# Attention and two MLPs on one core: PSUM banks held in pairs, weight pieces of 512 words, first scores one batch ahead, and MLP2's down weights decoded in the second phase

## The chip, the cores and the metric

One core of a Trainium2 chip runs the whole program. The metric is the device time of one execution in microseconds; lower is better. The kernel before was measured at 1560.72 us, the median of two executions (1560.45 and 1561.00).

## The reference, cut to what matters

```python
def sm_attn(qq, kk, vv):                    # scale = 1/8
    s = scale * np.matmul(qq, kk.transpose(0, 1, 3, 2))
    s = s - np.max(s, axis=-1, keepdims=True)
    a = np.exp(s)
    a = a / (np.sum(a, axis=-1, keepdims=True) + 1e-09)
    return np.matmul(a, vv)

p_packed = sm_attn(p, k, v)                 # 32 packed rows a head
out = sm_attn(q, p_packed, p_packed)        # (8, 8, 576, 64)

x = out.transpose(0, 2, 1, 3).reshape(4608, 512)
g = x @ w_gate                              # MLP1, d_ff 1536
x = (g * (1 / (1 + np.exp(-g))) * (x @ w_val)) @ w_out
h = x @ w_in                                # MLP2, d_ff 2048
y = (h * np.cos(h)) @ w_out2
```

The weights of both MLPs are float64. They arrive as pairs of 32-bit words and are turned into float32 on the chip. Where a product must keep float32's precision, an operand is split into a high and a low half (`split`: ACT copies to the high one, DVE subtracts to get the low one), and three matmuls replace one (`PASSES`).

## The kernel before, in words

**First phase, eight batches `b`.** `a_up(b)` (line 423) makes MLP1's gated hidden values for the 576 tokens of batch b: 12 columns `f` of 128 hidden units, each in two halves `c` of 288 tokens. A half has a gate product `pg` and a value product `pv`, in a bank of PSUM each (one pool `ps` of 8 banks). ACT evicts `pg` with silu (line 471), DVE multiplies it with `pv` into `h` (472), and POOL issues the store of `h` for both halves (479). The weights are multiplied with the packed values before (`a_wp`, line 408: two of the six 256-column groups `m` at a time, at f = 2, f = 6 and, for the next batch, in a side slot), so that the second attention's probabilities `a` can be multiplied with them directly. Batch 0 has no split operands and decodes the gate and value weights as it goes (`u_step`).

After every half a side slot `k = 2f + c` runs what the table `sched` holds. There are: the first scores of batch b+2 (`s1_mm` to `a_ppt`: p k^T, exp, times v, transposed), the second scores of batch b+1 (`s2_mm` to `s2_split`: q against the packed rows, softmax, split into `a`), loads of k, q, v, and `w2_step`: one step of the decode of the other weights, in pieces of 256 words. A piece is loaded by SP (`raw`, 328), decoded by two ACT operations (`w2t`, `w2f`: 98, 99) and two of DVE (105, 108), combined for Strassen's scheme (346), split (86, 87), and stored by SP (340) to `w1u` (MLP1's down weights), `w2u` (MLP2's up weights), and last to `w2d` (MLP2's down weights). The side slots of the last batch run two steps each. Engines work in program order, so what stands in a slot stands in front of the evictions behind it.

**Second phase.** MLP1's down product, as Strassen's seven products for each of five `SETS` of tokens (four with N = 512, one with N = 256). `prep` splits h (`hr`) into three `g` pieces for the next product (7 buffers); `sums1` makes differences of h quarters on DVE (534); `strassen(s_, i, m)` issues 18 matmuls for each half m, all three pieces `fp` for m = 0, then for m = 1, and `evict` adds up. DVE runs `sums1`, the low halves and the additions in that order. PE takes 7 x 36 matmuls a set.

**Third phase.** MLP2, whose functions `product`, `chain` and `down` the change does not touch.

Of the kernel before, what the change touches and what calls it, by code (L numbers as in the profile page):

```python
# [23 lines left out]
HS = S // 2  # L24
NP1 = NF1 // 2
NW1 = 2 * NP1
SETS = ((0, 512), (1024, 512), (2048, 512), (3072, 256), (3584, 512))
NC = -(-S // 128)
# [5 lines left out]
ATT = 24  # L34
ORDER = (0, 4, 6, 1, 3, 2, 5)
# [9 lines left out]
def attention_mlp_kernel(ctx: ExitStack, tc: tile.TileContext, qT, kT, vP, pP, wgv, w12, out):  # L45
# [5 lines left out]
    stage = {n: ExitStack() for n in ("ups", "att", "gates", "da", "db", "dw")}  # L51
# [7 lines left out]
    ps = ctx.enter_context(tc.tile_pool(name="ps", bufs=8, space=bass.MemoryType.PSUM))  # L59
# [11 lines left out]
    def wt(shape, dt, name):  # L71
        return ups.tile(shape, dt, tag="w", name=name, bufs=8)

    def bank(shape, name):
        return ps.tile(shape, F32, tag="b", name=name)
# [12 lines left out]

    def raw_words(alloc, src, n):
        r = alloc([128, n, 2], U32, "raw")  # L90
        SP.dma_start(out=r, in_=src.bitcast(U32).rearrange("p (n t) -> p n t", t=2))
        return r
# [19 lines left out]
    def keep_busy(n):  # L112
        wm = bank([128, 128], "wm")
        for _ in range(n):
            PE.matmul(out=wm, lhsT=zero, rhs=zero, start=True, stop=True)  # L115
# [26 lines left out]
    def pp_of(b, r, c):  # L142
        e, c1 = c % 2, 2 * (c // 2) + r
        return ppT[b, e][rows(r), cols(c1)]
# [3 lines left out]
    def s1_mm(b):  # L148
        sp = s1_["sp"] = [[bank([128, HS], "s1") for _ in range(2)] for _ in range(2)]
        for h in range(2):  # L150
            for c in range(4):
                for r in range(2):
                    PE.matmul(
                        out=sp[h][r][cols(c), :],
# [7 lines left out]
    def s1_max(r):  # L162
        mx = st.tile([128, 2], F32, tag="mx", name="mx")
        for h in range(2):
            DVE.tensor_reduce(out=mx[:, h:h + 1], in_=s1_["sp"][h][r], axis=AX.X, op=ALU.max)
        nm = s1_["nm", r] = st.tile([128, 1], F32, tag="nm", name="nm")
        DVE.tensor_scalar(
            out=nm, in0=mx[:, 0:1], scalar1=mx[:, 1:2], scalar2=-0.125, op0=ALU.max, op1=ALU.mult
        )

    def s1_exp():
        sp = s1_.pop("sp")
        for r in range(2):
            E[r] = at_([128, SPAD], F32, "E")
            nc.gpsimd.memset(E[r][:, S:SPAD], 0.0)
            sm = s1_["sm", r] = st.tile([128, 2], F32, tag="sm", name="sm")
            nm = s1_.pop(("nm", r))
            for h in range(2):
                ACT.activation(  # L179
                    out=E[r][:, HS * h:HS * h + HS], in_=sp[h][r], func=AF.Exp, scale=0.125,  # L180
                    bias=nm, accum_out=sm[:, h:h + 1],
                )

    def s1_sum():
        for r in range(2):
            rs[r] = st.tile([128, 1], F32, tag="rs", name="rs")
            sm = s1_.pop(("sm", r))
            DVE.tensor_scalar(
                out=rs[r], in0=sm[:, 0:1], scalar1=sm[:, 1:2], scalar2=1e-9, op0=ALU.add, op1=ALU.add
            )  # L190
            DVE.reciprocal(out=rs[r], in_=rs[r])

    def a_t():
        for r in range(2):
            e = E.pop(r)
            ET[r] = []
            for c0, n in ((0, 3), (3, 2)):
                tp = bank([128, n, 128], "tp")
                for c in range(n):
                    o = 128 * (c0 + c)  # L200
                    PE.transpose(out=tp[:, c, :], in_=e[:, o:o + 128], identity=ident)
                et = at_([128, n, 128], F32, "ET")
                ACT.activation(out=et, in_=tp, func=AF.Copy)
                ET[r].append(et)

    def a_pp(b):
        for r in range(2):
            et = ET.pop(r)
            pp = bank([128, 1, 64], "pp")
            for c in range(NC):  # L210
                for i in range(4):
                    PE.matmul(
                        out=pp[cols(i), 0, :],
                        lhsT=et[c // 3][:, c % 3, cols(i)],
# [5 lines left out]
                out=ppu[r], in0=pp.to_broadcast([128, 2, 64]), scalar1=rs.pop(r), scalar2=None, op0=ALU.mult  # L220
# [4 lines left out]
    def a_ppt(b):  # L225
# [799 lines left out]
```

## Time and profile before

| | us |
|---|---|
| median of two executions | 1560.72 |
| profiled execution | 1558.54 |
| its span | 1556.7 |
| PE busy in it | 1475.7 (95%) |
| DVE busy | 1117.6 (72%) |
| ACT busy | 866.0 (56%) |

A row of the trace gives start and length in us, engine, line, operation, tiles as out<-in, and in brackets how long the engine was idle before and what released it. SPq is SP's DMA queue, where the time is that of issuing. PEld are weight loads, which run beside the matmuls. The clock of PE is given as a share of its full speed. The stretches named here are: prologue to 24.9 us, batch 0 to 107.4, batches 1 to 6 to 431.4, the last batch to 508.0, the second phase to 802.0 (its first two products to 544.7), then the third phase.

### The profile page before, as it was taken

The page shows a single profiled execution, that of the slowest core. Times are in us where ns is not written, and L with a number is a line of the kernel's source. Part 1 is how long each engine was busy: PE and PEld are TensorE (multiplying, and loading weights), DVE is VectorE, ACT ScalarE, POOL GpSimd, SP SyncE. Part 2 cuts the span into 40 slices and gives each one's busy share as a digit, 9 for nine tenths or more (in the row PEclk, how much of TensorE's full clock was granted, in tenths as well). Part 3 has the DMA queues.
Part 4 walks back from the last instruction along what each step waited for, and adds up shares of the span by engine and source line. Part 5 has one row for each costly group of instructions (what it writes and reads, how often), then busy time and mean ns, then how long its engine had stood idle before and what let it go on. Part 6 is the DMA issues. An engine that isn't in the chain of part 4 may idle for free.

```text
span 1556.7 us, 26541 instructions
## 1 busy us (share of the span) xinstructions
PE 1475.7 (95%) x9452; PEld 1271.4 (82%) x9452; DVE 1117.6 (72%) x2139; ACT 866.0 (56%) x1847; POOL 76.3 (5%) x158
## 2 busy tenths in 40 slices
PE   9978999998966699999989999999999999999999
PEld 6657787787865588889888898999999999999987
DVE  6768898898855577677777676776686677577664
ACT  6766667667644343344447565555464655555552
POOL 0101111111100000001000000000000000000000
PEclk9999999999988899999999999999999999999999
DMA  9936787786678951535268666567558557656551
GB/s 344 344 118 234 257 308 262 275 288 231 212 260 269 321 196 65 210 112 185 89 243 285 209 197 226 184 213 256 168 180 286 189 165 245 225 185 190 191 164 45
DMA packets 160626, 335.72 MB, mean 216 GB/s; under 512 B 16880, under 2 KB 35312, under 8 KB 160496
## 3 DMA queue, kind: packets, MB, share of 16 engines
q1 hardware_dynamic: 149872, 296.28, 56.9%
q0 software_dynamic: 10624, 37.76, 6.2%
q8 instruction: 75, 1.23, 0.3%
q14 instruction: 55, 0.45, 0.1%
HBM read 252.71 MB, written 81.26 MB: 215 GB/s over the span
## 4 chain that ended last, share of the span: by engine, by line
PE 65%; issue 26%; POOL 3%; DVE 2%; ACT 2%; DMA 1%; POOLq 0%; SPq 0%; DVEq 0%; ACTq 0%
PE acc L888 25%; PE p L873 22%; PE o L557 16%; POOL h L479 3%; DMA hr<-h 0%; DMA raw<-in_wgv 0%; PE wm L115 0%; DMA h<-h 0%; PE pg L448 0%; PE pv L448 0%; DVE wg L105 0%; DVE xs L87 0%; ACT k L857 0%; ACT t L851 0%; ACT E L179 0%
## 5 line engine op out<-in xcount | busy, mean ns | idle before, releaser
L888 PE MATMUL acc<-wd,g 128*128 128x512 f32 x1728 | 418.1, 391 | 0.0
L873 PE MATMUL p<-xs,up 128*128 128x384 f32 x2016 | 381.3, 340 | 5.9 <-DMA up<-w2u 4.7
L873 PEld LDWEIGHTS p<-xs,up 128*128 128x128 f32 x2016 | 361.5, 189 | 17.5 <-issue 5.1
L888 PEld LDWEIGHTS acc<-wd,g 128*128 128x128 f32 x1728 | 323.1, 188 | 61.4
L557 PE MATMUL o<-g,w 128*128 128x512 f32 (+1 forms) x1260 | 267.4, 374 | 12.2 <-DVE g L87 10.5
L557 PEld LDWEIGHTS o<-g,w 128*128 128x128 f32 x1260 | 221.4, 190 | 57.9 <-DVE g L87 11.9
L851 ACT ACTIVATE t<-c,quarter 128x384 f32<-128x384 f32 x144 | 88.4, 614 | 200.8 <-DVE c L961 195.0
L463 PE MATMUL pg<-a,wp 128*128 128x288 f32 x1008 | 169.9, 304 | 28.6 <-ACT silu L471 14.9
L463 PEld LDWEIGHTS pg<-a,wp 128*128 128x128 f32 x1008 | 144.2, 191 | 54.1 <-ACT silu L471 20.0
L463 PE MATMUL pv<-a,wp 128*128 128x288 f32 x1008 | 163.9, 298 | 5.3 <-DVE h L472 4.3
L463 PEld LDWEIGHTS pv<-a,wp 128*128 128x128 f32 x1008 | 144.4, 190 | 8.5 <-DVE h L472 7.0
L86 ACT ACTIVATE g<-hr 128x1024 fp32r<-128x1024 f32 (+1 forms) x105 | 98.3, 968 | 70.6 <-DVE hr L534 46.5
L87 DVE TENSOR_TENSOR g<-hr,g 128x1024 fp32r<-128x1024 f32 (+1 forms) x105 | 113.3, 1113 | 22.4 <-ACT g L86 22.3
L956 DVE TENSOR_TENSOR u<-v,p 128x384 f32<-128x384 f32 x48 | 26.6, 554 | 121.1 <-PE p L873 120.8
L861 DVE TENSOR_TENSOR g<-t,g 128x384 fp32r<-128x384 f32 x192 | 106.0, 552 | 8.6 <-ACT g L848 8.5
L853 DVE TENSOR_TENSOR t<-t,k 128x384 f32<-128x384 f32 x192 | 106.1, 553 | 3.4 <-ACT k L857 1.8
L472 DVE TENSOR_TENSOR h<-silu,pv 128x288 f32<-128x288 f32 x192 | 85.8, 447 | 29.7 <-ACT silu L471 15.7
L471 ACT ACTIVATE silu<-pg 128x288 f32<-128x288 f32 x192 | 76.8, 407 | 46.6 <-PE pg L463 43.3
L854 ACT ACTIVATE t<-t 128x384 f32<-128x384 f32 x192 | 98.2, 512 | 2.5 <-DVE t L853 2.4
L848 ACT ACTIVATE g<-t 128x384 fp32r<-128x384 f32 x192 | 98.7, 514 | 0.4 <-DVE t L859 0.4
L902 DVE TENSOR_TENSOR oacc<-oacc,acc 128x512 f32<-128x512 f32 x108 | 73.8, 684 | 34.6 <-PE acc L888 34.6
L857 ACT ACTIVATE k<-t 128x384 int32<-128x384 f32 x192 | 98.0, 510 | 0.0
(97 smaller groups left out, 1504.5 us busy)
## 6 DMA issues: line engine op xcount, KB each, us to landing
up<-w2u SPq DMA_DIRECT2D x336, 256.0 KB, 3.1
wd<-w2d SPq DMA_DIRECT2D x96, 512.0 KB, 6.2
h<-h POOLq DMA_DIRECT2D x96, 288.0 KB, 4.0
hr<-h SPq DMA_DIRECT2D x48, 512.0 KB, 7.3
raw<-in_w SPq DMA_DIRECT2D x88, 256.0 KB, 4.0
w2u<-w2p SPq DMA_DIRECT2D x56, 256.0 KB, 3.6
raw<-in_wgv SPq DMA_DIRECT2D x24, 512.0 KB, 8.7
w1u<-w2p SPq DMA_DIRECT2D x42, 256.0 KB, 3.6
```

What stands on the lines that cost most here:

```text
L86: ACT.activation(out=hi, in_=src, func=AF.Copy)
L87: eng.tensor_tensor(out=lo, in0=src, in1=hi.bitcast(F32), op=ALU.subtract)
L463: PE.matmul(out=p_, lhsT=w[u][:, x, o:o + 128], rhs=a2[b, u][:, y, sl], start=(n == 0), stop=(n == 5),)
L557: PE.matmul(out=acc, lhsT=wd1[n, fp][:, j, 256 * x + 128 * m:256 * x + 128 * m + 128], rhs=g1[n, fp][:, y, j, :], start=(first and q == 0) ...
L848: ACT.activation(out=three["g"][:, 0, :], in_=three["t"], func=AF.Copy)
L851: ACT.activation(out=now["t"], in_=now["h"], func=AF.Identity, scale=1.0 / TWO_PI, bias=quarter)
L853: DVE.tensor_tensor(out=one_["t"], in0=one_["t"], in1=one_["k"], op=ALU.subtract)
L854: ACT.activation(out=one_["t"], in_=one_["t"], func=AF.Sin, scale=SIN_SCALE)
L857: ACT.activation(out=now["k"], in_=now["t"], func=AF.Copy)
L861: DVE.tensor_tensor(out=three["g"][:, 1, :], in0=three["t"], in1=three["g"][:, 0, :].bitcast(F32), op=ALU.subtract)
L873: PE.matmul(out=out, lhsT=w[:, u, 128 * k:128 * k + 128], rhs=x[:, v, k, :], start=(first and k == 0 and i == 0), stop=(last and k == 1 an ...
L888: PE.matmul(out=acc, lhsT=gs[p, a, t][:, x, o:o + 128], rhs=wd[j, f][:, y, :], start=(f == 0 and n == 0), stop=(f == 3 and n == 2),)
```

## The change

- **Bank pairs.** The pool `ps` holds four double banks [128, 2, 512]. `pg` and `pv` of both halves share one each, so one silu, one multiplication (128x576) evicts both; the same holds for scores, transposes and packed weights, and the second scores' softmax works on both 576-wide parts at once (128x1152). A group `m` of packed weights is made alone. The third phase opens a pool `ps1` of eight single banks.
- **Weight pieces of 512 words**, seven steps for a pair of pieces; their stores are issued by POOL, not SP. Batches 1 to 6 run 15 steps each, the last batch 8, all for `w1u` and `w2u`.
- **Scores one batch ahead.** `attention(sched, b + 1)` puts both scores of the next batch into batch b. The last batch and batch 0 hold no others.
- **MLP2's down weights** (16 items, 32 steps) are decoded in the second phase, one or two steps a product from product 3 of set 0 on.
- **Second phase.** The order of the products is 0, 4, 6, 1, 2, 3, 5; `strassen` takes the pieces `fp` outermost and both halves m within, into one double bank; `g` has 4 buffers; the loads of w1 and h and the three `prep` of product 0 are put into the last batch; the ten warm-up matmuls ahead of the phase leave. At the third phase's start the up weights take their tiles ahead of the down weights.

The core of the diff:

```diff
-ORDER = (0, 4, 6, 1, 3, 2, 5)
+ORDER = (0, 4, 6, 1, 2, 3, 5)
-    ps = ctx.enter_context(tc.tile_pool(name="ps", bufs=8, space=bass.MemoryType.PSUM))
+    ps = stage["ps"].enter_context(
+        tc.tile_pool(name="ps", bufs=4, space=bass.MemoryType.PSUM, reuse_waits="tile")
+    )
-    def bank(shape, name):
-        return ps.tile(shape, F32, tag="b", name=name)
+    def bank2(name):
+        return ps.tile([128, 2, 512], F32, tag="b", name=name)
...
+    def w2_put(w_, dst):
+        n = w_.shape[1]
+        p = w2_new([128, n, 2, 256], F32R, "p", "w2p")
+        split(w_, p[:, :, 0, :], p[:, :, 1, :])
+        nc.gpsimd.dma_start(out=dst.rearrange("n p c -> p n c"), in_=p.bitcast(F32).rearrange("p n x c -> p n (x c)"))
...
+        return [w2_decode(i), left, w2_decode(i + 1), sums_a, put_a, sums_b, put_b]
+
+    for n in range(NP1):
+        w2_todo += w2_pair(w1u[n], 2 * n)
+    for n in range(NPF):
+        w2_todo += w2_pair(w2u[n], NW1 + 2 * n)
+    for n in range(NF2):
+        w2_todo += [w2_decode(NW1 + NF2 + n), lambda n=n: w2_put_d(w2_f.pop(NW1 + NF2 + n), w2d[n])]
...
         for f in range(NF1):
+            pg = half(f, 0, "pg")
+            s_ = ups.tile([128, 2, HS], F32, tag="silu", name="silu", bufs=3)
+            ACT.activation(out=s_, in_=pg, func=AF.Silu)
+            side(2 * f)
+            pv = half(f, 128, "pv")
+            h_ = ups.tile([128, 2, HS], F32, tag="h", name="h", bufs=5)
+            DVE.tensor_tensor(out=h_, in0=s_, in1=pv, op=ALU.mult)
+            nc.gpsimd.dma_start(out=h1[f, :, S * b:S * b + S], in_=h_.rearrange("p c n -> p (c n)"))
+            side(2 * f + 1)
...
     def new_g(N):
-        n = g_n[0] % 7
+        n = g_n[0] % 4
...
         for fp in range(3):
-            for j in range(2):
-                for x, y in PASSES:
+            for m in range(2):
+                for j in range(2):
+                    for q, (x, y) in enumerate(PASSES):
...
+                for m, k in ((2, 2), (3, 5), (4, 9), (5, 14)):
+                    put(sched, k, lambda m=m: a_wp(b, m))
                 if b < B - 1:
+                    attention(sched, b + 1, (0, 1, 4, 4, 7, 8, 11, 12, 13, 13, 15, 16, 17, 18, 18, 21))
+                    for k in (1, 2, 3, 4, 5, 6, 7, 8, 9, 10, 19, 20, 21, 22, 23):
+                        put(sched, k, w2_step)
                 else:
-                    for k in range(24):
-                        put(sched, k, w2_step, w2_step)
-                    put(sched, 0, lambda: load_h(0, 0, 0), lambda: load_w1(0))
-                    put(sched, 6, lambda: load_h(0, 1, 0), lambda: load_h(0, 1, 1))
-                    put(sched, 20, lambda: prep(0, 0, 0))
-                    put(sched, 21, lambda: prep(0, 0, 1))
+                    for k in range(8):
+                        put(sched, k, w2_step)
+                    put(sched, 0, lambda: load_w1(0), lambda: g_first.append(new_g(512)), lambda: load_h(0, 0, 0))
+                    put(sched, 4, lambda: load_w1(4))
+                    put(sched, 8, lambda: load_h(0, 1, 0))
+                    put(sched, 12, lambda: load_w1(6))
+                    put(sched, 16, lambda: load_w1(1))
+                    for fp, k in enumerate((19, 21, 23)):
+                        put(sched, k, lambda fp=fp: prep(0, 0, fp))
...
-        prep(0, 0, 2)
-        load_w1(4)
-        load_w1(6)
+        load_h(0, 1, 1)
         load_h(0, 0, 1)
-        keep_busy(10)
         for s_ in range(len(SETS)):
             for i in range(7):
+                evict = strassen(s_, i)
                 sums1(s_, i)
+                for fp in range(3):
+                    prep(*nxt(s_, i), fp)
...
+                if s_ or i > 2:
+                    for _ in range(2 if i in (1, 6) else 1):
+                        w2_step()
...
+                evict()
```

Three places show what the change moves.

SP's DMA queue in the last batch, before: `raw` are loads of weight pieces, `w2d<-w2p` stores of decoded ones, `hr` loads of h for the second phase, `w_...<-w1u` loads of MLP1's down weights.

```order
L340 DMA w2d<-w2p 256x1x256
L505 DMA hr<-h_76 128x2x512 x3
L492 DMA w_6654<-w1u 128x2x512
L492 DMA w_6656<-w1u 128x2x512
L492 DMA w_6658<-w1u 128x2x512
L328 DMA raw<-in_w 128x512
L340 DMA w2d<-w2p 256x1x256
```

The same queue in the last batch of the change, up to the end of that batch, with the six loads of h that stand at the second phase's start as its last row:

```order
L513 DMA hr<-h_76 128x2x512 x3
L500 DMA w_5284<-w1u 128x2x512
L500 DMA w_5286<-w1u 128x2x512
L500 DMA w_5288<-w1u 128x2x512
L513 DMA hr<-h_76 128x2x512 x3
L500 DMA w_5459<-w1u 128x2x512
L500 DMA w_5461<-w1u 128x2x512
L500 DMA w_5463<-w1u 128x2x512
L500 DMA w_5539<-w1u 128x2x512
L500 DMA w_5541<-w1u 128x2x512
L500 DMA w_5543<-w1u 128x2x512
L513 DMA hr<-h_76 128x2x512 x6
```

Raw loads and stores have left the queue there.

ACT in the last batch, before: each silu has a weight piece's decode (98, 99) and split (86) in front of it.

```order
L471 ACTIVATE silu<-pg 128x288
L98 ACTIVATE w2t<-raw 128x256
L99 ACTIVATE w2f<-raw,low_87 128x256
L86 ACTIVATE w2p<-w2f 128x256
L86 ACTIVATE wp<-wp 128x512 x4
L471 ACTIVATE silu<-pg 128x288
L98 ACTIVATE w2t<-raw 128x256
```

ACT at the end of the last batch of the change: silus of 576 columns, the last packed weights (`wp`), and the splits of h for product 0 (`g`).

```order
L469 ACTIVATE silu<-pg 128x576
L86 ACTIVATE wp<-wp 128x2x512
L469 ACTIVATE silu<-pg 128x576 x3
L86 ACTIVATE wp<-wp 128x2x512
L469 ACTIVATE silu<-pg 128x576 x2
L86 ACTIVATE g<-hr 128x1024
L469 ACTIVATE silu<-pg 128x576
L86 ACTIVATE g<-hr 128x1024
```

No decode stands among the silus of the last two thirds any more.

DVE from the last batch's end into set 0 of the second phase, before: `h` is line 472, subtractions of h quarters are 534, low halves of `g` 87, evictions 577.

```order
L472 TENSOR_TENSOR h<-silu,pv 128x288 x2
L87 TENSOR_TENSOR g<-hr,g 128x1024
L534 TENSOR_TENSOR hr<-hr 128x1024 x3
L87 TENSOR_TENSOR g<-hr,g 128x1024 x5
L577 TENSOR_TENSOR x2e<-p,o_7520 128x512
L87 TENSOR_TENSOR g<-hr,g 128x1024
L577 TENSOR_TENSOR x2e<-p,o_7548 128x512
L534 TENSOR_TENSOR hr<-hr 128x1024 x3
```

The same place after the change: `h` is line 482, subtractions of h quarters are 542, evictions 575, weight steps 100 and 103 and `w2p`.

```order
L482 TENSOR_TENSOR h<-silu,pv 128x576
L87 TENSOR_TENSOR g<-hr,g 128x1024
L542 TENSOR_TENSOR hr<-hr 128x1024 x3
L87 TENSOR_TENSOR g<-hr,g 128x1024 x6
L575 TENSOR_TENSOR p<-p,o_5753 128x512 x2
L542 TENSOR_TENSOR hr<-hr 128x1024 x3
L87 TENSOR_TENSOR g<-hr,g 128x1024 x3
L542 TENSOR_TENSOR hr<-hr 128x1024 x3
L87 TENSOR_TENSOR g<-hr,g 128x1024 x3
L100 SCALAR_TENSOR_TENSOR w2f<-w2t,w2f 128x512
L103 SCALAR_TENSOR_TENSOR w2f<-raw,w2f 128x512
```

The three pieces of product 0 stand ahead of the phase's first subtractions now, and weight steps stand behind a product's three low halves.

## Rows read from the trace of the kernel before

**Rows 1.** Stretches: start:end, length, busy time of PE, PEld, DVE, ACT, POOL; clock; DMA; GB/s.

```profile
24.90:107.40 82.50, 71.95 (x681) 44.67 (x681) 59.77 (x120) 61.04 (x130) 6.57 (x15) 0.98 0.75 265
107.40:163.00 55.60, 51.68 (x544) 43.51 (x542) 45.30 (x111) 37.06 (x96) 6.44 (x14) 1.00 0.65 224
...
328.80:384.30 55.50, 51.58 (x543) 43.42 (x542) 48.53 (x122) 38.88 (x101) 6.75 (x15) 1.00 0.68 238
384.30:431.40 47.10, 46.54 (x419) 40.43 (x418) 41.89 (x98) 31.87 (x78) 6.23 (x12) 1.00 0.68 228
431.40:508.00 76.60, 49.67 (x353) 43.67 (x352) 39.12 (x93) 34.52 (x91) 6.49 (x12) 0.82 0.80 265
508.00:544.70 36.70, 23.54 (x93) 18.02 (x93) 19.31 (x25) 13.63 (x22) 1.62 (x3) 0.81 0.92 323
544.70:702.80 158.10, 158.10 (x685) 128.65 (x685) 116.46 (x112) 66.22 (x75) 11.90 (x22) 1.00 0.42 146
702.80:732.70 29.90, 29.90 (x254) 29.86 (x253) 24.89 (x41) 14.10 (x25) 4.12 (x8) 1.00 0.39 137
...
790.70:802.00 11.30, 6.59 (x23) 6.23 (x22) 4.67 (x7) 2.20 (x4) 0.55 (x1) 0.70 0.66 233
802.00:1556.70 754.70, 749.71 (x3725) 676.64 (x3723) 512.86 (x978) 417.80 (x886) 0.00 (x0) 1.00 0.62 204
```

**Rows 2.** Waits of PE in 431.4:508.0: waited for, us in total, times, longest.

```profile
PE pg L463 <- ACT silu L471: 14.5, 6, 12.0
PE pg L463 <- DVE wp L87: 11.9, 1, 11.9
```

**Rows 3.** Timeline of the last batch: start, length, engine, line, operation, idle before, releaser.

```profile
451.81 0.43 ACT L98 ACTIVATE w2t<-raw 128x256 f32<-128x256 f32 x1 [10.33 <-DMA raw<-in_w]
...
455.29 1.81 PE L463 MATMUL pg<-a,wp 128*128 128x288 f32 x6 [11.88 <-DVE wp L87]
...
479.73 0.43 ACT L98 ACTIVATE w2t<-raw 128x256 f32<-128x256 f32 x1 [11.13 <-DMA raw<-in_w]
...
482.29 1.81 PE L463 MATMUL pg<-a,wp 128*128 128x288 f32 x6 [12.02 <-ACT silu L471]
```

**Rows 4.** Timeline at the start of the second phase.

```profile
520.22 5.46 SPq L505 DMA_DIRECT2D hr<-h  x3
...
529.71 3.91 DVE L534 TENSOR_TENSOR hr<-hr 128x1024 f32<-128x1024 f32 x3 [10.76 <-DMA hr<-h]
...
534.81 5.41 PE L557 MATMUL o<-g,w 128*128 128x512 f32 x15 [8.94 <-DVE g L87]
```

**Rows 5.** Stretches: batches 1 to 6 in one row.

```profile
107.40:431.40 324.00, 304.96 (x3120) 257.67 (x3119) 280.40 (x688) 219.96 (x562) 39.62 (x81) 1.00 0.73 254
```

**Rows 6.** Instructions by line and shape: count, busy us, mean ns, idle before.

```profile
L472 DVE TENSOR_TENSOR h<-silu,pv 128x288 f32<-128x288 f32 x192 | 85.8, 447 | 29.7 <-ACT silu L471 15.7 <-PE pv L448 6.7 <-PE pv L463 5.3
...
L87 DVE TENSOR_TENSOR wp<-wp 128x512 fp32r<-128x512 f32 x84 | 52.0, 681 | 2.6 <-ACT wp L86 2.4
...
L87 DVE TENSOR_TENSOR a<-af,a 128x576 fp32r<-128x576 f32 x14 | 10.5, 752 | 1.5 <-ACT a L86 1.5
...
L87 DVE TENSOR_TENSOR g<-hr,g 128x1024 fp32r<-128x1024 f32 x84 | 99.7, 1220 | 20.3 <-ACT g L86 20.3
...
L87 DVE TENSOR_TENSOR g<-hr,g 128x512 fp32r<-128x512 f32 x21 | 13.7, 686 | 2.1 <-ACT g L86 2.0
...
L86 ACT ACTIVATE g<-hr 128x1024 fp32r<-128x1024 f32 x84 | 85.8, 1054 | 59.9 <-DVE hr L534 42.5 <-DMA hr<-h 10.6 <-PE o L557 5.1
...
L413 PE MATMUL wp<-wg,ppT 64*32 64x512 f32 x672 | 44.8, 597 | 7.1 <-ACT silu L471 7.1
...
L240 PE MATMUL s<-qt,ppT 64*32 64x288 f32 x256 | 10.4, 409 | 0.1
...
L471 ACT ACT_TABLE_LOAD x9 | 11.5, 1283 | 0.2
...
L179 ACT ACT_TABLE_LOAD x7 | 9.0, 1283 | 3.8 <-DVE nm L167 3.7
```

More of the change, by code (lines that the diff above doesn't have):

```diff
@@ L175, in s1_exp @@
             nc.gpsimd.memset(E[r][:, S:SPAD], 0.0)
[L176 to L182, printed above, removed]
+            sm = s1_["sm", r] = st.tile([128, 1], F32, tag="sm", name="sm")
+            ACT.activation(
+                out=E[r][:, :S].rearrange("p (h n) -> p h n", h=2), in_=sp[r][:, :, :HS], func=AF.Exp, scale=0.125,
+                bias=s1_.pop(("nm", r)), accum_out=sm,
+            )
     def s1_sum():
@@ new lines, in s2_back, with s2_split @@
+    def s2_back(b, u=None):
+        if "af" not in s2_:
+            s2_["af"] = att.tile([128, 2, S], F32, tag="af", name="af", bufs=2)
+        to, d_ = s2_["af"], s2_["d"]
+        if u is None:
+            DVE.transpose(out=to, in_=d_.rearrange("p (u a) n -> p u (a n)", u=2))
+        else:
+            DVE.transpose(out=to[:, u], in_=s2_d(u).rearrange("p a n -> p (a n)"))
+    def s2_split(b):
+        a2[b] = s2_["af"]
+        if b:
+            a2[b] = ups.tile([128, 2, 2, S], F32R, tag="a2", name="a2", bufs=2)
+            split(s2_["af"], a2[b][:, :, 0, :], a2[b][:, :, 1, :])
+        s2_.clear()
@@ L375, in w2_work, with w2_new @@
[L375 to L390 removed]
+    NITEM = NW1 + 2 * NF2
+    w2_end = [NW1 + NF2]
+    w2_bufs = {"r": (ups, 3), "s": (ups, 7), "p": (ups, 3)}
+    def w2_new(shape, dt, tag, name):
+        where, bufs = w2_bufs[tag]
+        return where.tile(shape, dt, tag="w2" + tag, name=name, bufs=bufs)
@@ L398, in a_wp0 @@
                 PE.matmul(
[L399 removed]
+                    out=p_[cols(c), r, :256],
                     lhsT=pp_of(0, r, c),
@@ new lines, in keep, with plus @@
+        def keep(m):
+            o_ = late["db"].tile([128, N], F32, tag="t", name="p", bufs=8)
+            ACT.activation(out=o_, in_=acc[:, m, :N], func=AF.Copy)
+            return o_
+        def plus(o_, x, y):
+            DVE.tensor_tensor(out=o_, in0=x, in1=y, op=ALU.add)
+        def evict():
+            for m in range(2):
+                if n in (0, 1, 2, 3):
+                    part[n, m] = keep(m)
+                if n == 4:
+                    o_ = part.pop((0, m))
+                    plus(o_, o_, acc[:, m, :N])
+                    x2_store(s_, 0, 0, m, o_)
+                elif n == 3:
+                    w_, c22 = part.pop((3, m)), part.pop((2, m))
+                    plus(c22, w_, c22)
+                    x2_store(s_, 1, 1, m, c22)
+                    plus(w_, w_, acc1[2][:, m, :N])
+                    x2_store(s_, 0, 1, m, w_)
+                elif n == 5:
+                    o_ = part.pop((1, m))
+                    plus(o_, o_, acc[:, m, :N])
+                    x2_store(s_, 1, 0, m, o_)
```

527 lines of the change are left out of this document (223 added, 304 removed).

## The prediction

> **What bounds the kernel now.** I read the stretches first. In them the reader is to see where TensorE (PE) is busy for the whole stretch and where it is not. From 544.7 us on it is: 158.10 of 158.10 us, 29.90 of 29.90, and 749.71 of 754.70 in the third phase [rows 1]. Nothing can be won there without taking matmuls away, and the change takes none. Idle PE time lies ahead of that: 10.6 us in batch 0, 3.9 in batches 1 and 5, 27 in the last batch, 13 at the start of the second phase and 4.7 where the third phase begins [rows 1]. The last batch is the worst, and two of its waits hold nearly all of the 27 us: 11.9 and 12.0 us [rows 2]. They name VectorE (DVE) and ScalarE (ACT), but the timeline shows what is behind them: ACT had waited 10.33 and 11.13 us for a raw piece of the weights (the decode of MLP2's down weights), and the eviction or the silu that PE wanted stood behind that decode in ACT's order [rows 3]. In the second phase's start it is a DMA again: a load of h issued at 520.22 released the subtractions at 529.71 after 10.76 us, and PE's second product started 8.94 us late [rows 4]. So what is to be had is 27 + 20 us of waits for transfers, and little else.
>
> The profiled execution took 1558.54 us, 1.8 outside its span; the median of the two runs is 1560.72, 2.2 above it. Sums go against 1558.54, and 2.2 is added at the end.
>
> **1. Batch 0.** The first scores of batch 2 leave it. What they cost PE is read from batch 6, which has none: 46.54 us busy against 51.58 in batch 5, so 5.0 [rows 1]. Of the 10.6 us idle I give back 4, since ACT and DVE lose the scores' evictions too: **-9** (-14 all of it, -4 if the pairs keep PE waiting as long as now).
>
> **2. Batches 1 to 6.** They take 324.00 us now [rows 5], with batch 6 at 47.10 because it holds no first scores [rows 1]. After the change each of the six holds a whole attention, so batch 6 gains those 5.0 us. DVE: `h` becomes 12 operations of 128x576; the nearest row of that width is the 752 ns of the low half of `a`, against 447 ns for 128x288 [rows 6], so a pair saves 2 x 447 - 752 = 142 ns, a fixed cost paid once. A packed weight's low half becomes 1024 wide: 1.22 us as `g`, against 2 x 0.681 [rows 6]. Per batch DVE has 12 x 0.75 + 6 x 1.22 + attention about 13.6 (each operation of before at double width, less 0.145) + 15 weight steps. Seven steps are two decodes of 2 x 0.69, and 512-wide work for about 4.1: 6.9 us, so 15 take 14.8. The sum is 44.7, against 48.5 in batch 5 [rows 1]. PE's work is 51.6 as in batches 1 to 5. Idle PE was 3.9 in batch 1 and in batch 5; with DVE 3.8 lighter I take 2.9: 6 x 54.5 = 327, **+3**. Below: 1.0 idle, 316 (-8). Above: four double banks instead of eight single ones, and the table loads, rivals A and C (+27).
>
> **3. Last batch.** The decode of MLP2's down weights leaves it; 8 weight steps remain in its first third, whose raw pieces were loaded in batch 6. SP's queue, which carried a raw load and a store for each piece between the loads of h and `w1u`, now holds only the latter, and stores go out on POOL's queue, which carries `h`. With no raw load in flight, ACT has nothing to wait for. PE's work is that of batch 6 less the second scores (10.4 us in eight batches, 1.3) and less two packed weights (44.8 us for 42, 1.07 each) [rows 6]: 46.54 - 1.3 - 2.1 = 43.1, and 1.5 idle: 44.6 against 76.60 [rows 1], **-32** (-28 to -34).
>
> **4. Start of the second phase.** 36.70 us hold two products and the gaps before them [rows 1]. A product is 158.10 / 19 = 8.32 us [rows 1], so 20 us are excess. After: product 0's three `g` are made inside the last batch, and PE starts at once. Product 1 stands in DVE's order behind three subtractions on h(0,1), which can be loaded only when the last batch's memory comes free: six loads of 0.52 MB at the 323 GB/s of that stretch [rows 1] take 9.7 us, then 1.22 and 1.22 [rows 6]: 12.2, against 8.3 of product 0, so PE waits 3.9 us. With 1.2 more for the half clock that followed such waits (0.81 of the clock in that stretch) 5 us remain: **-15** (-10 to -18).
>
> **5. Second phase, steady.** The moved decode is 32 steps of 1.03 us DVE on average (1.38 or 0.69), 9 in a set from product 3 of set 0 to the end of set 3. An N=512 set has 33 operations of 1.22, 8 evictions of 0.69 [rows 6] and now 9.3 us of steps: 55 us against 7 x 8.32 = 58.2. That is hidden by PE, with under 1 us to spare in the products that subtract. In the N=256 set it isn't: 33 x 0.686 [rows 6] + 8 x 0.42 + 9.3 = 35.3 against 29.90 [rows 1], +5.4. With 2 for late first pieces: **+7** (0 if DVE catches up in the last set, +16 if each subtracting product shows 0.5).
>
> **6. Start of the third phase.** PE is busy 6.59 of 11.30 us [rows 1], since the up loads wait for memory of the last product. Their tiles are now taken first, and the operands of the last product come free piece by piece, as its matmuls run piece after piece: **-5** (-2 to -6). The third phase keeps its instructions: 0. The prologue: 0.
>
> Sum: -9 + 3 - 32 - 15 + 7 - 5 = -51; 1558.5 - 51 + 2.2 = **1510 us**.
>
> **Weighed against a rule.** Table loads are counted at 1.283 us each, and the 16 that serve silu and the first exp [rows 6] stand beside idle ACT time (38.88 of 55.50 busy in batch 5) [rows 1]. The changed program has 30 where there were 20 in all, since each batch has two stretches of exp; in the sum they cost nothing. The Trainium skill, page "ScalarE: Activation LUTs", section "What ACT_TABLE_LOAD costs", says a switch takes a drain of about 1.38 us besides the load, about 2.66 in all. By that rule the ten would be 26.6 us of ACT, and an estimate by it, were all on the path, is 1537 us. The trace shows the load's 1.283 us; it doesn't show a drain as a row of its own.
>
> **Rivals.**
> A. *Pairs bind PE to its evictors.* A bank pair is free only after an operation on both halves, and there are four. PE fills one in about 1.6 us; first scores, second scores and packed weights each hold one or two while DVE, in order, may have 1.2 to 2.5 us of other work ahead. If each batch shows 4.5 us more than my 2.9 (say three such waits of 1.5), it is +27: 1537. For it: PE's idle time in a batch is put down to silu and `h` already. Against it: DVE is the lighter by 3.8 us. The Trainium skill, page "Perfetto Trace Analysis", section "Matmuls", wants independent groups to rotate through different banks, so that one is evicted under the next group's matmuls; it speaks for A, and no row of before shows fewer than eight banks.
> B. *The other side: four tiles of `g` make the second phase serial.* A piece's split (high half about 1.05, low half 1.22 [rows 6]) can begin only when the piece of the running product is done. If the first piece of the next product comes L late in each of 35 products, it costs 35 L. Without the loss it would be -58; slower by over 2% needs 35 L > 89, L = 2.6 us, which is one high and one low half exposed. At L = 2.6, 1594 us. Against it: the first piece takes the fourth tile, which has been free since the product before, and its deadline is 8.3 us on; DVE has 6.3 us ahead of it at most.
> C. *The ten table loads lie on the path:* 10 x 1.283 = +12.8: 1523. For it: in the first stretch of a batch scores, exp and the silu that PE waits for lie close together. Against it: ACT has 16 us idle in a batch.
> D. *The change doesn't free the last batch:* one of its two waits comes back, since loads of h and `w1u` stay there and transfers already ran at 0.80 [rows 1]. +12: 1522. Against it: nothing in the batch needs a load until its last six columns.
>
> **Numbers.** Forecast 58% (1495 to 1525), A 14%, C 12%, D 9%, B 5%, 2% for something else. Two per cent, about what a measurement can tell from no change, is 31 us: faster below 1529.5, slower above 1592. The forecast, C, D and a little of A are faster: 80%. The rest of A and the something else are within 2%: 15%. B is slower: 5%. The range runs from 1488 (batch 0, batches and second phase at their good ends) to 1538, which takes in A.
>
> **What the profile after would show.** The last batch 43 to 46 us with no idle PE over 3 us. Batch 6 longer, by 5 to 8 us, the others 53 to 56. At the start of the second phase one PE wait of 2 to 6 us on DVE, behind a load of h. DVE over 95% busy in the N=256 set, and PE with a few us idle there; elsewhere in the phase PE waits under 0.5 a product. The prediction is wrong if waits for silu, `h` or packed weights sum to over 8 us in a batch, or if PE waits for `g` in every product.

## The result, and the profile after

The changed kernel takes 1522.18 us (median of 1522.15 and 1522.20), 38.5 us less than before: the ratio is 0.9753, with a 95% interval of 0.9711 to 0.9795. The forecast was 1510 with a range of 1488 to 1538. Its profiled execution has a span of 1520.4 us against 1556.7.

Stretches of the changed kernel: start:end, length, busy time of PE, PEld, DVE, ACT and POOL, granted clock, DMA share, GB/s. The rows are batch 0, batches 1, 4 and 6, the last batch, the first two products of the second phase, and the set of N = 256.

```profile
26.05:96.84 70.79, 64.78 (x558) 41.90 (x557) 53.12 (x82) 52.94 (x82) 6.33 (x13) 0.98 0.82 288
96.84:152.62 55.78, 52.12 (x542) 43.29 (x540) 38.20 (x59) 31.53 (x46) 10.05 (x19) 1.00 0.57 207
268.35:327.37 59.02, 53.20 (x543) 44.67 (x541) 42.28 (x65) 34.35 (x52) 12.78 (x24) 0.97 0.63 229
385.41:442.10 56.69, 51.81 (x543) 43.18 (x542) 42.29 (x65) 33.49 (x49) 12.58 (x24) 1.00 0.68 231
442.10:485.76 43.66, 43.40 (x354) 39.10 (x353) 25.63 (x38) 20.00 (x30) 11.69 (x20) 1.00 0.87 335
485.76:503.90 18.14, 16.73 (x74) 13.34 (x73) 12.47 (x11) 7.54 (x9) 0.54 (x1) 1.00 1.05 396
662.90:696.20 33.30, 30.41 (x250) 29.61 (x249) 30.37 (x51) 21.84 (x40) 6.18 (x12) 1.00 0.72 253
```

The last batch has PE busy for 43.40 of 43.66 us, where it was busy for 49.67 of 76.60 [rows 1]. The batches ahead of it went the other way: 55.8 to 59.0 us each, batch 6 included, against 55.5 for batch 5 and 47.1 for batch 6 [rows 1]. In batches 3 and 4 the clock is 0.97, so it was at half for a while. Batches 1 to 6 in one row, as [rows 5]:

```profile
96.84:442.10 345.26, 313.99 (x3243) 262.03 (x3242) 246.78 (x378) 198.11 (x287) 74.06 (x133) 0.99 0.64 228
```

That is 345.26 us for 324.00. PE's waits in it (what it waited for, us in total, times, longest):

```profile
PE pp L195 <- DVE ppu L202: 10.4, 6, 2.1
PE wp L425 <- ACT silu L469: 7.0, 5, 1.8
PE tp L185 <- DVE wp L87: 5.6, 6, 1.4
PE pv L456 <- DVE h L482: 4.9, 5, 1.5
PE wp L425 <- DVE wp L87: 1.9, 1, 1.9
```

The forecast's terms and what the two profiled executions show, in us (spans; 1556.7 to 1520.4):

| part | forecast | measured | how read |
|---|---|---|---|
| prologue | 0 | +1.1 | first column starts at 26.05, was 24.90 |
| 1. batch 0 | -9 | -11.7 | 70.79 for 82.50 |
| 2. batches 1 to 6 | +3 | **+21.3** | 345.26 for 324.00 |
| 3. last batch | -32 | -32.9 | 43.66 for 76.60 |
| 4. first two products | -15 | -18.6 | 18.14 for 36.70 |
| 5, 6. rest of the second phase, with the start of the third | +7 - 5 | +4.4 | 255.47 for 251.10 |
| third phase | 0 | +0.1 | 761.03 for 760.90 |
| sum | -51 | -36.3 | |

The short set of the second phase and what comes behind it, in the changed kernel. SPq rows are SP's queue (start and time of issuing):

```profile
663.65 17.58 SPq L335 DMA_DIRECT2D raw<-in_w  x3
...
682.55 1.89 DVE L87 TENSOR_TENSOR g<-hr,g 128x512 fp32r<-128x512 f32 x3
683.26 11.61 SPq L513 DMA_DIRECT2D hr<-h  x12
...
706.64 0.49 PE L562 MATMUL o<-g,w 128*128 128x512 f32 x1 [2.16 <-ACT g L86]
...
707.90 51.62 PE L562 MATMUL o<-g,w 128*128 128x512 f32 x215 [0.77 <-DVE g L87]
```

Raw pieces of the decode are on SP's queue from 663.65 to 681.23, and the loads of h for the last set stand behind them. They start at 683.26, 0.71 us after the start of the splits on DVE that read the tiles of h to be filled again. The second product of the last set waits 2.16 and 0.77 us for its first `g`.

### The profile page after: what moved, and what is told of

It reads as the page before. It is cut to its first block, busy times and chain, and to the rows that moved or that the text cites. A ratio compares the mean times of both kernels' runs of the same rounds, so it can differ in the third digit from the quotient of the medians.

```text
span 1520.4 us, 25197 instructions
## 1 busy us (share of the span) xinstructions
PE 1465.4 (96%) x9432; PEld 1262.3 (83%) x9432; DVE 1087.6 (72%) x1767; ACT 850.2 (56%) x1501; POOL 123.9 (8%) x230
## 4 chain that ended last, share of the span: by engine, by line
PE 65%; issue 7%; DVE 5%; DMA 3%; ACT 3%; POOL 1%; SPq 0%; POOLq 0%; DVEq 0%; ACTq 0%
PE acc L891 26%; PE p L876 22%; PE o L562 14%; PE pg L456 2%; PE pv L456 1%; DMA hr<-h 1%; POOL h L483 1%; DMA w<-w1u 1%; DVE h L482 1%; POOL w2u L344 1%; DMA w2u<-w2p 1%; DVE wp L87 0%; DVE w2f L100 0%; PE wp L425 0%; DVE p L575 0%
## 5 line engine op out<-in xcount | busy, mean ns | idle before, releaser
L456 PEld LDWEIGHTS pv<-a,wp 128*128 128x128 f32 x1008 | 138.7, 189 | 26.3 <-DVE h L482 7.6
L86 ACT ACTIVATE g<-hr 128x1024 fp32r<-128x1024 f32 (+1 forms) x105 | 102.0, 976 | 101.4 <-PE o L562 54.1
L456 PE MATMUL pv<-a,wp 128*128 128x288 f32 x1008 | 152.7, 301 | 5.5 <-DVE h L482 4.9
L456 PEld LDWEIGHTS pg<-a,wp 128*128 128x128 f32 x1008 | 138.8, 189 | 21.1 <-issue 8.3
L456 PE MATMUL pg<-a,wp 128*128 128x288 f32 x1008 | 152.5, 300 | 0.3 <-DVE h L482 0.3
L469 ACT ACTIVATE silu<-pg 128x576 f32<-128x576 f32 x96 | 62.3, 649 | 82.8 <-PE pg L456 70.5
L87 DVE TENSOR_TENSOR wp<-wp 128x1024 fp32r<-128x1024 f32 x42 | 51.3, 1221 | 51.8 <-ACT wp L86 51.7
## 6 DMA issues: line engine op xcount, KB each, us to landing
w<-w1u SPq DMA_DIRECT2D x21, 512.0 KB, 11.2
```

Source lines behind the costliest of these rows:

```text
L86: ACT.activation(out=hi, in_=src, func=AF.Copy)
L87: eng.tensor_tensor(out=lo, in0=src, in1=hi.bitcast(F32), op=ALU.subtract)
L456: PE.matmul(out=p_[:, c, :HS], lhsT=w[:, u, x, o:o + 128], rhs=a2[b][:, u, y, HS * c:HS * c + HS], start=(n == 0), stop=(n == 5),)
```

## The experiments

Ten kernels ran: single edits of the changed kernel or of the kernel before first, then repairs put together.

### Both halves of pp before their evictions

In the changed kernel `pp` holds both r in one double bank. The timeline shows what that does: the first product of `pp` ends at 117.3, its eviction `ppu` stands on DVE behind an `h` (and that behind weight steps), and the second product starts when it is done.

```profile
116.57 0.77 PE L195 MATMUL pp<-vt,ET 128*32 128x64 f32 x40
...
117.30 0.75 DVE L482 TENSOR_TENSOR h<-silu,pv 128x576 f32<-128x576 f32 x1
...
117.96 0.34 DVE L202 TENSOR_SCALAR ppu<-pp,rs 128x128 f32<-128x128 f32 x1
...
118.36 0.77 PE L195 MATMUL pp<-vt,ET 128*32 128x64 f32 x40 [1.03 <-DVE ppu L202]
```

```diff
         pp = bank2("pp")
         for r in range(2):
             ...
                     PE.matmul(out=pp[cols(i), r, :64], ...)
+        for r in range(2):
             ppu[r] = st.tile([128, 2, 64], F32, tag="ppu", name="ppu", bufs=2)
             DVE.tensor_scalar(out=ppu[r], in0=pp[:, r:r + 1, :64]...)
```

> One edit on the changed kernel: both halves of pp (r = 0 and r = 1, two halves of one double bank) are multiplied before either is evicted, instead of multiply, evict, multiply, evict. In the changed kernel PE waits 10.4 us in six batches for the eviction of the first half (ppu) before it starts the second, in batches 1 to 6. Theory 1 (a pair is held as one tile, so a write into its other half waits for the eviction of the first; this is what the pairs cost): the wait row goes, batches 1 to 6 take 9 to 12 us less, the total falls to 1509 to 1513. Theory 2 (DVE and ACT, in order, set the pace of a batch, and the wait only shows where PE meets them): the wait comes back at ppt, wp or pv, the total falls by under 4 us, to 1518 or more.

Measured: 1510.67 us, ratio to before 0.9688 (0.9674 to 0.9702), apart from the changed kernel's. Batches 1 to 6:

```profile
95.91:430.25 334.34, 313.33 (x3243) 260.66 (x3242) 246.51 (x378) 198.09 (x287) 73.97 (x133) 0.99 0.66 237
```

The wait row of 10.4 us is gone and the batches take 10.9 us less. No other wait row grew by more than 0.1 us. So theory 1 holds: the second half was multiplied late only because a pair is one tile, and a write to its other bank waited until the first had been read. The loss was in the order of the code, not in the engines.

### The decode's work left out

```diff
-        w2_todo += w2_pair(w1u[n], 2 * n)          # and the same for w2u
+        w2_todo.append(lambda: nc.gpsimd.dma_start(out=w1u[n, j], in_=kT[...]))
```

> The decode of MLP1's down and MLP2's up weights is left out of batches 1 to 7 (their ACT and DVE operations and raw loads); at the same slots POOL issues copies of as many bytes from k into w1u and w2u, so what these weights are is changed, and the stores' traffic remains. DVE loses 14.7 us and ACT 11 us of work a batch. Theory 1 (the waits of batches 1 to 6 come from work that stands ahead of evictions in DVE's and ACT's order): the 31 us of waits there fall to under 10 us, a batch takes 52 to 54 us instead of 57.5, in sum 312 to 325 for 345. Theory 2 (four double banks are too few, whatever the engines do): at least 20 us of waits stay, sum 335 or more.

Measured: 1497.17 us, ratio 0.9603 (0.9588 to 0.9617). Batches 1 to 6, and PE's waits in them:

```profile
96.38:413.00 316.62, 308.42 (x3240) 258.92 (x3239) 171.16 (x229) 143.58 (x186) 86.66 (x171) 1.00 0.62 207
```

```profile
PE wp L429 <- ACT silu L473: 5.2, 6, 0.9
PE pp L195 <- DVE ppu L202: 3.0, 6, 0.5
```

A batch takes 52.8 us, 1.4 above PE's 51.4, with the same four pairs, the same evictions and the same table loads. Theory 1 holds, and theory 2 falls: four pairs are enough when the decode isn't in the way. What made PE wait was the decode's operations, which stand in DVE's and ACT's order ahead of an eviction; even the wait at pp shrinks to 0.5 us each. The raw loads left with them, but they aren't the cause: in the changed kernel ACT's waits in batches 1 to 6 name no raw load.

### MLP2's down weights back in the last batch

```diff
-    w2_end = [NW1 + NF2]
+    w2_end = [NITEM]
...
-                    for k in range(8):
-                        put(sched, k, w2_step)
+                    for k in range(20):
+                        put(sched, k, w2_step, w2_step)
...
-                if s_ or i > 2:                    # second phase
-                    for _ in range(2 if i in (1, 6) else 1):
-                        w2_step()
```

> One part of the change is undone: MLP2's down weights are decoded in the last batch again (two steps in each of its first twenty slots, pieces of 512 words, stores on POOL's queue), and none in the second phase. Theory 1 (the last batch was long because ACT stood at decodes whose raw loads came late among h and w1u): the last batch takes 60 to 75 us instead of 43.7, with PE waits over 5 us behind raw loads, the rest of the second phase 6 to 10 us less; total 1530 to 1548. Theory 2 (pieces of 512 words and stores off SP's queue have already cured it, and the move is worth nothing): last batch under 50 us, total 1516 to 1524.

Measured: 1565.40 us, ratio 1.0032 (1.0019 to 1.0045): the whole gain is lost. The last batch:

```profile
441.65:530.66 89.01, 56.82 (x354) 47.54 (x352) 55.70 (x84) 46.54 (x76) 19.61 (x35) 0.82 1.00 379
```

It takes 89.0 us, more than either theory said, and its DMA share is 1.00 over the whole batch, where the last batch before had 0.80 [rows 1]. In the changed kernel the gain hangs on the move; what the move alone gives on the kernel before was not run. Theory 1's reason was too narrow: ACT waited 4.8 us for raw pieces here and 11.2 for stores to leave their tiles, and PE's waits are under 3.4 us each. The batch moves 33.7 MB, where the last batch before moved 20.3, since the changed kernel has also put the weights of four products there. At the 412 GB/s of its best 15 us these bytes alone would take 82 us, an estimate.

### The same with another order of the steps

```diff
-    for n in range(NF2):
-        w2_todo += [w2_decode(...n), lambda n=n: w2_put_d(...n)]
+    for n in range(NF2 + 1):
+        if n < NF2:
+            w2_todo += [w2_decode(...n)]
+        if n:
+            w2_todo += [lambda n=n - 1: w2_put_d(...n)]
```

> e3 (MLP2's down weights decoded in the last batch) with the order of its steps changed, so that a slot decodes one piece and stores the piece decoded in the slot before; in e3 a slot decodes and splits the same piece, so that ACT and DVE wait for each other four times a slot. In e3 the last batch takes 87 us, at a DMA share of 0.98 to 1.01 all through. Theory 1 (transfers fill the last batch: raw pieces, stores, h and all of w1u's loads share it, some 30 MB): the batch stays at 80 us or more, total 1558 to 1568. Theory 2 (the two engines' order in a slot is the limit): the batch falls under 70 us, total under 1548.

Measured: 1566.18 us, ratio 1.0039 (1.0028 to 1.0049). (The last batch of the run before it is 89.0 us by its row, not the 87 of the expectation.) The order within a slot is worth nothing:

```profile
443.57:534.69 91.12, 58.96 (x355) 51.40 (x353) 54.25 (x84) 46.05 (x76) 19.61 (x35) 0.78 0.95 356
```

DMA is at 0.95 and the batch takes 91.1 us. Theory 2 falls; the run agrees with theory 1. ACT's waits for raw pieces are back at what they were in the last batch of the kernel before (first row: the kernel before; second row: this run), while in the changed kernel's last batch ACT has no such row:

```profile
ACT w2t L98 <- DMA raw<-in_w: 22.1, 4, 11.1
ACT w2t L93 <- DMA raw<-in_w: 22.1, 7, 8.3
```

That the transfers alone set the length isn't shown by it: the clock is low in that stretch as well.

### First scores one ahead, alone, on the kernel before

```diff
-                first_scores(sched, b + 2, (6, 7, 8, 9, 14, 17, 19))
-                second_scores(sched, b + 1, (0, 1, 2, 3, 5, 6, 8, 9, 10, 11, 13, 12, 13, 14, 15, 20))
+                first_scores(sched, b + 1, (0, 1, 2, 3, 4, 7, 8))
+                second_scores(sched, b + 1, (10, 11, 12, 13, 13, 14, 14, 15, 16, 17, 18, 16, 17, 18, 19, 21))
```

> One part of the change alone on the kernel before: first scores one batch ahead, at slots close to those of the changed kernel; single banks, pieces of 256 words and all else stay. Theory 1 (this move only shifts first scores out of batch 0 and into batch 6, as the prediction had it): batch 0 takes 5 to 14 us less, batch 6 7 to 9 us more, batches 1 to 5 stay near 55.4; total 1554 to 1564. The excess of batches 1 to 6 in the changed kernel (57.5 us each) is then the pairs'. Theory 2 (both scores in one batch, in a row, make the batch longer by themselves): batches 1 to 6 take 57 us or more with single banks too, total 1565 to 1575.

Measured: 1571.17 us, ratio 1.0075 (1.0060 to 1.0090). Batches 1 to 6, and PE's longest waits:

```profile
96.06:443.15 347.09, 323.87 (x3242) 262.38 (x3241) 287.46 (x701) 239.16 (x587) 40.38 (x84) 1.00 0.71 245
```

```profile
PE tp L201 <- DVE wp L87: 8.5, 6, 1.7
```

Packed weights on PE in batches 1 to 6, in the kernel before and in this run:

```profile
L413 PE MATMUL wp<-wg,ppT 64*32 64x512 f32 x576 | 38.2, 597 | 6.6 <-ACT silu L471 6.6
L413 PE MATMUL wp<-wg,ppT 64*32 64x512 f32 x576 | 53.0, 613 | 12.0 <-DVE h L472 9.9 <-ACT silu L471 1.9
```

347.09 us, 57.8 a batch, 23 us more than before; batch 0 gives 11.7 back. Of the 23, 5.0 are the first scores that batch 6 now holds [rows 1], so about 18 are loss. Theory 2 holds for these slots: packing a whole attention into one batch makes the batch longer by itself, with eight single banks and the old pieces too. The loss isn't all in idle time, which grew by only 4.2 us: the same 576 matmuls of the packed weights are drawn out over 53.0 us instead of 38.2. The wait at the transposes (`tp`, 8.5) and those at the packed weights (11.8) stand at the places where the changed kernel waits as well. Other slots for this move were not run on the kernel before.

### First scores two ahead again, in the changed kernel

On the first experiment: first scores of b + 2 in slots 11 to 19, second scores of b + 1 in slots 0 to 8, weight steps in 9 to 23.

> On e1, one part of the change undone: first scores stand two batches ahead again, first scores of batch b+2 in slots 11 to 19 and second scores of batch b+1 in slots 0 to 8 of batch b, weight steps in slots 9 to 23, one more buffer for ppT. Theory 1 (batches grew because the whole chain of one attention stands in one batch, each step a wait after the step before, as the kernel before grew by 11.7 us with this move alone): batches 1 to 5 take 1 to 3 us less than e1's 55.7 on average, batch 6 6 to 8 us less, batch 0 8 to 11 us more; total 1498 to 1510. Theory 2 (with pairs there is no difference, or four pairs can't hold both chains at once): batches 1 to 5 as in e1 or longer; total 1511 to 1522.

Measured: 1513.35 us, ratio 0.9707 (0.9692 to 0.9721), in theory 2's range. The stretches say otherwise, batch 0 and batches 1 to 6:

```profile
26.05:101.63 75.58, 67.67 (x682) 44.37 (x681) 56.04 (x92) 58.73 (x91) 6.59 (x15) 1.00 0.82 294
101.63:424.02 322.39, 309.38 (x3119) 258.61 (x3118) 244.42 (x369) 194.28 (x278) 73.94 (x131) 0.99 0.63 228
```

Batches 1 to 6 take 322.39, 11.95 us less than in the first experiment, and batch 0 takes 75.58 for 70.29: theory 1's direction, net -6.7, as some 5 us of first scores only change their batch. The total didn't follow, since a wait of 5.2 us came up at the start of the third phase and the second phase was 2.6 us longer. That wait is the subject of the last experiment.

### Four slots moved

```diff
-attention(sched, b + 1, (0, 1, 4, 4, 7, 8, 11, 12, 13, 13, 15, 16, 17, 18, 18, 21))
+attention(sched, b + 1, (0, 1, 4, 5, 7, 8, 11, 12, 13, 13, 15, 16, 17, 20, 20, 22))
```

> On e1 (both halves of pp before their evictions): the slots of four steps of attention(b+1) are moved. The transposes a_t go from slot 4 to 5, the split of the second scores from 18 to 20 and the packed weights m = 0 and 1 from 18 and 21 to 20 and 22, so that silu of column 10 no longer stands on ACT behind the split, which waits for DVE. In e1 PE waits 7.0 us for silu at the packed weights, 5.7 us for the low half of packed weights at the transposes and 1.9 us more, in six batches. Theory 1 (PE's waits in batches 1 to 6 come from what stands ahead of an eviction in an engine's order, so they can be moved by slots): these rows fall by 8 to 12 us, total 1499 to 1504. Theory 2 (ACT and DVE are that full that a wait only changes its name): other rows grow by as much, total 1508 to 1513.

Measured: 1507.34 us, ratio 0.9669 (0.9653 to 0.9685), which overlaps the first experiment's. Batches 1 to 6 and PE's waits there:

```profile
95.47:421.20 325.73, 313.17 (x3242) 262.49 (x3241) 244.80 (x378) 198.06 (x287) 74.07 (x132) 0.99 0.67 240
```

```profile
PE pg L457 <- DVE h L483: 5.3, 3, 2.0
...
PE wp L426 <- DVE wp L87: 0.3, 1, 0.3
```

The three rows that were aimed at (7.0, 5.7 and 1.9) are down to 0.3, the others grew from 6.2 to 11.8, and the batches take 325.73 for 334.34. So theory 1 holds for the batches, though two fifths of the waits came back under other names. The total lies between the two forecasts: it fell by less, because the same 5.2 us came up at the third phase's start.

### No weight steps in the short set

```diff
-                if s_ or i > 2:
-                    for _ in range(2 if i in (1, 6) else 1):
+                if (s_ or i > 2) and s_ != 3:
+                    for _ in range(2 if i in (1, 4, 6) else 1):
```

> On the changed kernel, without e1: the weight steps of the second phase are kept out of the short set (N = 256) and spread over the others (one more at product index 4 of each, six in the last set). The changed kernel takes 33.3 us for that set against 29.9 before, and then waits 2.9 us for h at the second product of the last set, where loads of h had stood in SP's queue behind raw loads for 17.6 us. Theory 1 (prediction's term 5: the decode doesn't fit DVE in the short set, it is hidden elsewhere): the set is back to 30 to 31 us, the wait after it is gone, total 5 to 7 us less: 1515 to 1517. Theory 2 (the cost moves along, since DVE is at 95% in the long sets too): waits for g appear in sets 1, 2 and 4, total 1520 to 1524.

Measured: 1514.97 us, ratio 0.9727 (0.9703 to 0.9751). The interval overlaps the changed kernel's; the rows of PE in the second phase tell them apart:

```profile
485.87 8.58 PE L562 MATMUL o<-g,w 128*128 128x512 f32 x37
496.20 171.26 PE L562 MATMUL o<-g,w 128*128 128x512 f32 x756 [1.76 <-DVE g L87]
668.68 84.11 PE L562 MATMUL o<-g,w 128*128 128x256 f32 x467 [1.22 <-DVE g L87]
```

Three rows are all there is: one wait of 1.76 at the second product, one of 1.22 at the short set's start, and from there none to the third phase. The whole phase takes 266.8 us (485.87 to 752.63) for 273.6. Theory 1 holds, but the late h wasn't due to SP's queue, against what the expectation says. Here no raw load is near, and the loads of h still start 0.72 us after the start of the splits that read their tiles, as they did in the changed kernel (0.71):

```profile
679.22 1.29 DVE L87 TENSOR_TENSOR g<-hr,g 128x512 fp32r<-128x512 f32 x2
679.94 11.25 SPq L513 DMA_DIRECT2D hr<-h  x12
```

DVE comes to these splits 3.3 us earlier without the steps (679.22 for 682.55).

### All three, and the turn of the banks

> e5 and e6 together (pp before its evictions, slots moved, no weight steps in the short set). If the three are independent, as theory 1 of each has it, their gains add: 11.5 + 9 + 6 = 26 us under the changed kernel's 1522, total 1493 to 1499. If they share a limit (DVE or ACT over the whole), the sum is under 18 us, total over 1504.

Measured: 1499.06 us, ratio 0.9618 (0.9604 to 0.9633): 23 us under the changed kernel, just above the 1499 up to which the gains were to add, and what is missing to the full sum is again a wait at the third phase's start. PE there waits for no row that the profile names, but starts 0.11 us after the last evictions of the second phase on DVE, which stand behind the splits of the third phase's operands:

```profile
735.00 1.28 DVE L576 TENSOR_TENSOR p<-p,o 128x512 f32<-128x512 f32 x2
...
736.39 1.94 PE L877 MATMUL p<-xs,up 128*128 128x384 f32 x5 [5.16 <-issue]
```

The double bank of the last product's accumulators was the one that the third phase's first accumulator takes. In the changed kernel it was another pair. The programs as built bear this out: the third phase starts in bank 0, and the last accumulator lies in banks 0 and 1 in the five variants that wait there, in banks 2 and 3 in the changed kernel and the four that don't. Some of the five differ from the changed kernel only in code that uses no bank, so which pair it will be can't be seen from the edit.

```diff
+                if end and i == 4:
+                    keep_busy(1)                   # takes one double bank
                 evict = strassen(s_, i)
```

> e7 and one dummy matmul ahead of product index 4 of the last set, which shifts the turn of the double banks by one. In e7 the first accumulator of the third phase falls into the bank pair of the second phase's last product, whose eviction stands on DVE behind the splits of the third phase's operands, and PE waits 5.2 us there; in the changed kernel it falls into another pair and PE doesn't wait. Theory 1 (the turn of the pairs decides it): the wait goes, total 4 to 5.5 us under e7's 1499.1, 1493.5 to 1495.5. Theory 2 (PE waits there for something else): 1498 to 1500.

Measured: 1494.62 us, ratio 0.9585 (0.9571 to 0.9600), apart from the interval without it. Batches 1 to 6, the second phase; then the start of the third:

```profile
95.04:419.29 324.25, 311.70 (x3242) 260.99 (x3241) 244.75 (x378) 198.09 (x287) 73.94 (x132) 0.99 0.67 241
462.41:730.96 268.55, 265.54 (x1264) 220.81 (x1263) 230.35 (x257) 147.89 (x196) 29.84 (x55) 0.99 0.59 212
```

```profile
730.96 4.23 PE L879 MATMUL p<-xs,up 128*128 128x384 f32 x23
...
734.89 0.68 DVE L576 TENSOR_TENSOR p<-p,o 128x512 f32<-128x512 f32 x1
```

The wait is gone and theory 1 holds. This version beats both kernels: by 4.2% the one before and, by the two ratios, by 1.7% the changed one.

## Why the prediction was right, and where not

**Right in direction and range, high in gain.** The sum forecast -51, and -36.3 is measured in the spans. Terms 1, 3, 4, and 5 taken with 6, are within 4 us each; term 2 is off by 18. The other rows came out 3.6 us better in sum, which hid a little of that.

**Term 3, the last batch: size right, reason borne out, parts not told apart.** -32 forecast, -32.9 measured, by the route that was worked out (PE's matmuls plus a little idle). ACT's 22.1 us of waits for raw pieces are gone from that batch, and they return in one of the two runs that put the decode back. In the other they are 4.8 us, with 11.2 for stores, and the batch is as long: with 32 to 34 MB in it, it is long in either order. Both runs cost 45 us or more there, which is not the price of the old batch with its 20.3 MB. How much of the -32.9 is the move, and how much the wider pieces and the stores on POOL's queue, stays open.

**Term 2, batches 1 to 6: the step that failed.** I took 2.9 us idle a batch because DVE's work fell to 44.7 us. It fell further, to 41.1 (246.78 in six batches), the wide operations cost what was reckoned (`h` 128x576 took 747 ns for 752), and PE was still idle or slowed for 5.9 us over 51.6. A sum of busy time says nothing on when an eviction comes to its turn. Rival A had the place, nearly the price (4.5 more a batch forecast, 3.0 measured) and part of the cause: it had evictions stand behind other work of DVE, and without the decode's work a batch takes 52.8 us with the same four pairs. But it put the price on the pairs, and waits at the same places come with eight single banks too. Three things turned that into waits: a pair written and read by halves while it counts as one tile (10.9); the whole chain of an attention in one batch, so that each step is wanted a few slots after the one before (about 18 on the kernel before; 12 back when undone, 6.7 with what batch 0 then takes); and splits that wait for DVE in front of a silu on ACT (part of the 8.6 that the slots gave back). The last two are cures of the same waits and can't be added. With the first and the third cured the batches take 325.73 us, under the 327 of the forecast: the work was sized right, its order wasn't looked at.

**Term 1: batch 0.** -11.7 for -9: PE's work fell by 7.2 us, where 5.0 were taken for the first scores, and the idle 10.6 by 4.5. With one ahead alone it is the same -11.7, so it is this move that pays there. In batches 0 to 6 the move cost more than it gave as long as the slots stood as they were: undoing it won 6.7 us there on the first experiment. With the slots moved these batches take 395.8 us, against 398.0 with the move undone.

**Term 4: start of the second phase.** The wait I named came, in its place (product 1 behind three subtractions of h(0,1)), with 1.41 us instead of 3.9, and no half clock:

```profile
479.58 3.29 SPq L513 DMA_DIRECT2D hr<-h  x6
...
490.25 2.36 DVE L542 TENSOR_TENSOR hr<-hr 128x1024 f32<-128x1024 f32 x2 [2.34 <-DMA hr<-h]
...
495.77 16.43 PE L562 MATMUL o<-g,w 128*128 128x512 f32 x69 [1.41 <-DVE g L87]
```

The six loads were issued from 479.58, 6.2 us ahead of the phase's first matmul at 485.76, and the stretch moved 396 GB/s instead of the 323 that I took. The gain is a little beyond that term's range. No run separates what the loads, the three `prep` and the leaving of the warm-up matmuls gave.

**Term 5: second phase.** The long sets hide the decode, as said. The short set lost 3.4 us (33.30 for 29.90), for 5.4, and the next set's h came late by 2.9 more, where 2 were taken for late first pieces. Both are DVE's lateness in the short set, as the run without steps there shows. In all PE's waits come to 5.8 us behind the second product. Without steps in the short set they are 1.2.

**Term 6: third phase's start.** The 4.7 us are gone, with the up loads issued at 738.59 instead of 793.11. That it came out so cleanly was luck, a matter of which bank stood at its turn: five of the variants have a 5.2 us wait at that place for another reason. I had no term for it.

**Rivals.** B doesn't show: waits for `g` come to 5.8 us behind the second product, in one set and the product behind it. C doesn't either: the two loads that batch 1 has around its second exp stand at 130.83 and 135.44, and PE has no wait there, between those at 118.36 and 148.16. With all table loads in place and no decode work a batch is 1.4 us over PE's work. D is answered by 43.40 of 43.66.

**The signs that were named.** Right: the last batch, the short set's waits, the long sets but for the start of the last one. Neither sign of a wrong prediction came: PE's waits in batches 1 to 6 sum to 31.1 us, 5.2 a batch, where over 8 was named, so that sign was set too high to show term 2's miss. Wrong: batches 1 to 5 (55.8 to 59.0 for 53 to 56), batch 6 (+9.6 for 5 to 8), the wait at the second product (1.41 for 2 to 6), DVE in the short set (91% for 95%).

## What to carry to other kernels

Before code is moved for the engines' sums, read which eviction stands behind what in each in-order engine: here a batch of 57.5 us came down to 54 with the same operations and as many banks, by moving four slots and one loop. Where two halves share one buffer, write both before either is read, and look at which buffer the next phase's first tile falls into. A decode that can be put anywhere belongs where the transfers and the evicting engines have room: here not the last batch, and not the short set.

## What the runs showed of the hardware

Half clock came after short waits too, though not after each. In batch 3 PE waited 1.41 and 0.56 us within 4 us, and the next twelve matmuls took 3.25 us where twelve take 1.85; the granted clock of that stretch (223.9 to 227.3) was 0.52, with 0.98 ahead of it and 1.00 behind. A longer wait in the same batch, the 2.12 us at pp that ended at 234.38, had a clock of 1.00 behind it (234.38 to 239.00). The rows of batch 3:

```profile
222.59 0.77 PE L185 MATMUL tp<-ident,E 128*128 128x128 f32 x5 [1.41 <-DVE wp L87]
223.92 3.25 PE L456 MATMUL pv<-a,wp 128*128 128x288 f32 x12 [0.56 <-DVE h L482]
...
228.12 1.85 PE L456 MATMUL pg<-a,wp 128*128 128x288 f32 x12
```

```profile
223.90:227.30 3.40, 3.38 (x20) 3.08 (x28) 2.40 (x9) 2.05 (x5) 1.74 (x3) 0.52 0.54 206
```

A switch of ACT's tables took no more than the load. In the run without decode work the last exp's accumulator read ends at 103.53, the load stands at 103.55 for 1.28 us, and silu starts at 104.84, so the drain that the prediction weighed as a rule has no time here:

```profile
103.33 0.20 ACT L169 ACTIVATION_READ_ACCUMULATOR E<-s,nm 128x1 f32 x1
103.55 1.28 ACT L473 ACT_TABLE_LOAD   x1
104.84 0.65 ACT L473 ACTIVATE silu<-pg 128x576 f32<-128x576 f32 x1
```
